# DeltaNet and low-rank mixer on one core: K of the later units loaded in 32x32 blocks, word pairs in the small triangles, and a new order of instructions

## The chip, the cores and the metric

The kernel runs on one core of a Trainium2 chip. A core has five engines that run beside each other, each in the order of its own instruction stream: TensorE (PE in the profile, its weight loads PEld), VectorE (DVE), ScalarE (ACT), GpSimd (POOL) and SyncE (SP). DMAs are issued from the streams of SP, POOL and ScalarE. TensorE writes to PSUM, and the other engines bring its results to SBUF. The metric is the device time of one execution in microseconds (us).

## The reference

Two blocks follow one another. The first is the delta rule for 4 batches, 8 heads, 768 tokens and a head size of 48: with k normalised, each token reads y from a 48 x 48 state and then corrects the state.

```python
for t in range(S):
    kt, vt, bt = (k_n[:, :, t], v[:, :, t], beta[:, :, t, None])
    y[:, :, t] = np.einsum('bhd,bhde->bhe', q[:, :, t], state)
    v_old = np.einsum('bhde,bhd->bhe', state, kt)
    state = state + bt[:, :, :, None] * np.einsum('bhd,bhe->bhde', kt, vt - v_old)
```

Its output, as x of shape (4, 768, 384), goes through a mixer over tokens of rank 32 and two dense layers with a residual:

```python
h = xt @ U @ V
u = x + h.transpose(0, 2, 1)
ch = np.maximum(u @ w_ch1, 0.0) @ w_ch2
return (u + ch).astype(np.float32)
```

## The kernel before

The tokens of a batch are cut in 12 chunks of 64. A **unit** is half a batch: 6 chunks of all 8 heads. There are 8 units, n = 0 to 7; two slots of SBUF hold the operands of the units in turn (`slots[n % 2]`), so that unit n can be loaded when unit n - 2 has been used up (the `need` at L302).

For a unit, `load` brings K, Q and V with tokens on the partitions (`kn`, `qn`, `vn`), and a second copy of K's odd heads on the other half of the partitions (`kz`, name 'z'). The products of a chunk with itself need K and Q turned, with the head's dimension on the partitions (`kq`). K of all units, and Q of units 0 and 1, are turned by TensorE with `transpose`, a half of a unit at a time (`turn`, 12 transposes, L221), and ScalarE copies the result out of PSUM (L412). Q of units 2 to 7 is loaded in blocks of 32 x 32 (16 columns in the second block of a head) by L320, and one VectorE instruction turns half a unit (`turn_blocks`, L421).

`products` multiplies K by K and K by Q (L432). From K by K, the two diagonal blocks of 32 x 32 of each 64 x 64 square go to `diag`: ScalarE writes the upper one (L436), and VectorE adds the lower one with a mask (L439). `blocks` then inverts the triangles. VectorE lays `diag` out with one triangle to each partition (L484), scales it, and substitutes column by column in `xt` (L493 and L494, a product and a subtraction in each of 31 steps; in units 0 to 2 the triangles are split once more, so there are 15 steps). L498 transposes the result back into `zz`, L505 turns its blocks, and small matmuls on 32x32 tiles of the array (L586 to L599, "joins") complete the 64 x 64 inverse in `pg`.

`recur` runs through the chunks of a batch in order. Each chunk needs the state before it, and sums the new state on VectorE (L745). `put` writes y to X. The mixer of a batch follows in three groups of 256 tokens: `front` (L948, L1074), `wide` (first dense layer, L1151 on the whole array or L209 in four quarters) and `narrow` (second layer, with seven products in place of eight, L1239 or L209). The last batch's first layer is done for all its tokens with fifteen products in place of eighteen (L929). The weights are converted by VectorE and ScalarE at the start (L834 to L843).

Each of these parts is a Python generator. It yields before each step, naming the step's engine and, for TensorE, the kind of array tile (`mode`: F whole array, H half of the rows, Q quarters, J 32x32 tiles, T column strips). The string `ORDER` names the generators by number, one token for each step, and `run` advances them in that order. Each engine's instructions stand in this order, so ORDER fixes what waits behind what. A token with the letter q picks the quarter form of a dense step, and digits after a dot pick the PSUM banks.

## Time and profile before

| | us |
|---|---|
| median of 3 runs | 578.34 |
| lowest and highest | 577.12 and 578.95 |
| profiled execution | 580.21 |
| its span, first to last instruction | 578.5 |
| TensorE busy | 542.4 |
| VectorE busy | 417.7 |
| ScalarE busy | 239.6 |
| POOL busy | 112.2 |

The page has busy times of the engines, the span in 40 slices, the chain of work that ended last, groups of equal instructions and DMA issues. The trace can be asked for the same by stage, and for single instructions. A group's row gives the line, engine and operation, the output and input tile, shapes and count, and then the busy time in us, the mean of one instruction in ns, and the engine's idle time ahead of the group. TensorE runs each fp32 matmul of the program as two in the profile, while a transpose is one. Durations of single matmuls overlap, so TensorE is read by distances from start to start.

### The profile page before, as it was taken

The page shows a single profiled execution, that of the slowest core. Times are in us where ns is not written, and L with a number is a line of the kernel's source. Part 1 is how long each engine was busy: PE and PEld are TensorE (multiplying, and loading weights), DVE is VectorE, ACT ScalarE, POOL GpSimd, SP SyncE. Part 2 cuts the span into 40 slices and gives each one's busy share as a digit, 9 for nine tenths or more (in the row PEclk, how much of TensorE's full clock was granted, in tenths as well). Part 3 has the DMA queues.
Part 4 walks back from the last instruction along what each step waited for, and adds up shares of the span by engine and source line. Part 5 has one row for each costly group of instructions (what it writes and reads, how often), then busy time and mean ns, then how long its engine had stood idle before and what let it go on. Part 6 is the DMA issues. An engine that isn't in the chain of part 4 may idle for free.

```text
span 578.5 us, 24970 instructions
## 1 busy us (share of the span) xinstructions
PE 542.4 (94%) x11205; PEld 457.4 (79%) x11205; DVE 417.7 (72%) x1018; ACT 239.6 (41%) x515; POOL 112.2 (19%) x193
## 2 busy tenths in 40 slices
PE   4476899999999999999999999999999999999997
PEld 4476787669789788789879977989889769656997
DVE  5799876889899337999898789998733345556532
ACT  2777787533422554146135333522352321435100
POOL 8041133530201350501107205120010000000000
PEclk9999559999999999999999999999999999999999
DMA  9977565440200150610405315020000000000001
GB/s 139 189 161 199 147 181 112 73 87 2 71 14 2 25 106 8 117 32 2 87 7 87 84 22 93 6 68 3 31 3 2 32 2 1 27 0 1 27 15 42
DMA packets 73835, 33.37 MB, mean 58 GB/s; under 512 B 60416, under 2 KB 71808, under 8 KB 73728
## 3 DMA queue, kind: packets, MB, share of 16 engines
q1 hardware_dynamic: 66400, 23.21, 18.4%
q0 software_dynamic: 5728, 8.27, 7.0%
q8 instruction: 88, 1.44, 1.1%
q10 hardware_dynamic: 1600, 0.30, 0.3%
q14 instruction: 19, 0.16, 0.1%
HBM read 27.03 MB, written 4.72 MB: 55 GB/s over the span
## 4 chain that ended last, share of the span: by engine, by line
PE 85%; DVE 6%; DMA 2%; ACT 2%; issue 2%; SPq 1%; ACTq 0%; DVEq 0%
PE P L1239 25%; PE P L1151 15%; PE P L209 10%; PE P L929 7%; PE P L432 4%; PE P L976 3%; PE P L653 2%; PE P L711 2%; PE P L646 2%; PE P L739 2%; PE P L698 2%; DMA slot<-in_k_dram 2%; PE P L221 1%; PE P L948 1%; PE P L1074 1%
## 5 line engine op out<-in xcount | busy, mean ns | idle before, releaser
L1151 PE MATMUL P<-ut,w_sb 128*128 128x256 f32 x384 | 88.0, 384 | 0.0
L1151 PEld LDWEIGHTS P<-ut,w_sb 128*128 128x128 f32 x384 | 71.4, 190 | 10.5 <-issue 0.6
L1239 PE MATMUL P<-w_sb,hs 128*128 128x192 f32 x456 | 79.1, 329 | 0.1
L1239 PEld LDWEIGHTS P<-w_sb,hs 128*128 128x128 f32 x456 | 74.2, 190 | 2.4 <-issue 1.4
L494 DVE TENSOR_TENSOR xt<-xt,prod 128x112 f32<-128x112 f32 (+21 forms) x200 | 64.6, 323 | 6.9
L493 DVE TENSOR_TENSOR prod<-gs,xt 128x112 f32<-128x112 f32 (+21 forms) x200 | 63.7, 318 | 3.7
L1185 DVE TENSOR_TENSOR X<-X,P 128x192 f32<-128x192 f32 x85 | 29.5, 349 | 42.9 <-PE P L1239 39.5
L1121 ACT ACTIVATE hs<-P 128x512 f32<-128x512 f32 x48 | 28.7, 598 | 66.3 <-PE P L1151 50.5
L209 PE MATMUL P<-ut,w_sb 64*64 64x256 f32 x768 | 51.8, 382 | 0.0
L1239 PE MATMUL P<-w_sb,S 128*128 128x192 f32 x240 | 41.9, 329 | 0.0
L432 PE MATMUL P<-slot 48*64 48x64 f32 x1536 | 33.3, 243 | 9.1 <-ACT slot L412 7.8
L636 ACT COPY X<-P 64x192 f32<-64x192 f32 x96 | 30.1, 314 | 25.1 <-PE P L653 23.7
L327 POOL DMA_DIRECT2D slot<-in_k_dram x44 | 29.7, 678 | 55.6 <-PE P L739 54.8
L432 PEld LDWEIGHTS P<-slot 48*64 48x64 f32 x1536 | 30.4, 156 | 12.3 <-ACT slot L412 8.6
L1239 PEld LDWEIGHTS P<-w_sb,S 128*128 128x128 f32 x240 | 38.9, 190 | 1.1 <-issue 0.6
L320 POOL DMA_DIRECT2D slot<-in_q_dram x48 | 29.6, 621 | 42.5 <-DVE z L729 25.2
L616 POOL MEMSET slot<- 32x384 f32 x32 | 13.2, 412 | 118.6 <-PE P L587 117.4
L612 ACT COPY slot<-zz 32x384 f32<-32x384 f32 x64 | 32.6, 509 | 4.3 <-DVE zz L568 1.7
L1239 PE MATMUL P<-w_sb,slot 128*128 128x192 f32 x180 | 30.4, 327 | 0.9 <-DVE X L1185 0.9
L209 PEld LDWEIGHTS P<-ut,w_sb 64*64 64x64 f32 x768 | 25.6, 133 | 7.1 <-issue 0.6
L914 DVE TENSOR_TENSOR slot<-slot,P 128x384 f32<-128x384 f32 x36 | 19.1, 552 | 16.3 <-PE P L929 15.4
L1239 PEld LDWEIGHTS P<-w_sb,slot 128*128 128x128 f32 x180 | 29.3, 190 | 1.7 <-DVE X L1185 1.5
(185 smaller groups left out, 1001.3 us busy)
## 6 DMA issues: line engine op xcount, KB each, us to landing
w_sb<-in_moe_w_ch_dram SPq DMA_DIRECT2D x14, 384.0 KB, 5.9
out_dram<-X SPq DMA_DIRECT2D x22, 192.0 KB, 2.0
slot<-in_k_dram SPq DMA_DIRECT2D x48, 72.0 KB, 4.0
slot<-in_k_dram POOLq DMA_DIRECT2D x44, 72.0 KB, 3.7
slot<-in_v_dram SPq DMA_DIRECT2D x32, 72.0 KB, 3.6
slot<-in_v_dram POOLq DMA_DIRECT2D x32, 72.0 KB, 3.4
X<-in_moe_w_ch_dram SPq DMA_DIRECT2D x6, 384.0 KB, 5.2
wide<-in_moe_w_ch_dram SPq DMA_DIRECT2D x4, 384.0 KB, 4.9
```

The source lines that it names most:

```text
L209: nc.tensor.matmul(to[half(g)], w[half(r), half(g)], x[half(r)], start=start, stop=stop, skip_group_check=True)
L320: queue.dma_start(out=blocked(n)[quarter(2 * par + y), j, g, :, 0:cols.stop - cols.start], in_=of[:, :, cols])
L327: queue.dma_start(out=t[half(1 - g if name == 'z' else g), :, to, 0:D], in_=src[b, 4 * g + s, hf * UC * L:(hf + 1) * UC * L, :].rearrange( ...
L432: nc.tensor.matmul(p_g[half(g ^ par * i), par, c], kq[rows, c, j, 0, half(g)], kq[rows, c, j, i, half(g)], start=True, stop=True)
L493: nc.vector.tensor_tensor(out=prod, in0=gb[:, :, j:j + 1, j + 1:].to_broadcast([128, split, m, w]), in1=xb[:, :, 0:m, j:j + 1].to_broadcas ...
L494: nc.vector.tensor_tensor(out=xb[:, :, 0:m, j + 1:], in0=xb[:, :, 0:m, j + 1:], in1=prod, op=ALU.subtract)
L612: nc.scalar.copy(pg[quarter(i), :, at, :, a:a + BK], cut(zc, h)[quarter(i)].rearrange('p r (c j) t -> p r c j t', j=2))
L636: nc.scalar.copy(x[half(c % 2), c // 2, 4 * D * g:4 * D * (g + 1)].rearrange('p (j r d) -> p r j d', r=2, d=D), states(p_y)[half(g)])
L929: nc.tensor.matmul(banks[x], w1_sb[:, 4 * a[0] + e, a[1]] if isinstance(a, tuple) else w1_mixes[a][:, e], tokens(*t) if isinstance(t, tupl ...
L1151: nc.tensor.matmul(p_f[:, x], w(x, t), ut[:, t], start=t == 0, stop=t == KT - 1)
L1185: nc.vector.tensor_tensor(out=to, in0=to, in1=p, op=ALU.add)
L1239: nc.tensor.matmul(to, of[0], of[1], start=of[2], stop=of[3], skip_group_check=True)
```

## The change

K of units 2 to 7 is loaded a second time, in 32x32 blocks (name 'kb', 16 DMAs for a unit), into the place that `pg` takes later, and VectorE turns it, half a unit at a time, as it does Q. TensorE's transposes of K and ScalarE's copies for these units are gone. The plain load of K puts the odd heads on the other half of the partitions, so that the second copy ('z', 4 DMAs for a unit) is not loaded for these units. The copy of the products into `pg` waits until both halves of K are turned.

`diag` and `zc` hold the triangles of two heads as adjacent words (`r` innermost), and with them the lines that write and read them; L484 and L498 then step over pairs of words. The substitution works on `xt` with its two axes exchanged. From unit 3 on (`LIGHT`), ScalarE writes both diagonal blocks, the lower one with two copies of 32 partitions, in place of a masked write by ScalarE and two masked additions by VectorE. Steps of `norms` and of the substitution that were issued together are steps of their own in ORDER, and the diagonal of `xt` is written by a product in place of a copy. ORDER is new as a whole.

The diff, with unchanged lines and most of ORDER left out:

```diff
@@ -37,6 +37,7 @@
+    LIGHT = 3
@@ -50,98 +51,107 @@
-    0 1 0 149 1 0 1 37 0 1 2 2 21 147 21 37 14.0 36 37 36 22 36 201 201 22 36 39 15.1 38 37 38 39 148 202.2
 ...
-    711 711
+    0 1 0 150 1 149 0 1 2 0 1 37 37 36 37 36 22 14.0 36 22 36 2 213 213 21 39 2 38 37 15.1 21 39 38 39 214.2
 ...
+    706 706 702 707 700 703 708 703 709 709 704 710 710 698 711 711
@@ -249,17 +259,20 @@
-        diag = slot[:, 6144:6144 + BK * BK].rearrange('p (q t) -> p q t', t=BK)
+        diag = slot[:, 6144:6144 + BK * BK].rearrange('p (e t r) -> p e t r', t=BK, r=2)
 ...
-    def blocked(n):
-        return slots[n % 2][:, 7680:9216].rearrange('p (j g x t) -> p j g x t', j=2, g=2, t=BK)
+    def blocked(n, i):
+        return slots[n % 2][:, 7680:9216] if i else slots[n % 2][:, 4608:6144]
+
+    def in_blocks(n, i):
+        return blocked(n, i).rearrange('p (j g x t) -> p j g x t', j=2, g=2, t=BK)
 ...
-        nc.gpsimd.memset(units[i][6][:, CS:], 0.0)
+        nc.gpsimd.memset(units[i][6][:, CS // 2:], 0.0)
@@ -274,7 +287,7 @@
-    zc = zz[:, 0:CS * BK].rearrange('p (q t) -> p q t', t=BK)
+    zc = zz[:, 0:CS * BK].rearrange('p (e t r) -> p r e t', t=BK, r=2)
@@ -297,8 +310,10 @@
-        t, src = dict(k=(kn, k), q=(qn, q), v=(vn, v), z=(kz, k))[name]
+        t, src = dict(k=(kn, k), q=(qn, q), v=(vn, v), z=(kz, k), kb=(None, k))[name]
 ...
+        if name == 'z' and n >= NU:
+            return
@@ -310,21 +325,21 @@
-            if name == 'q' and n >= NU:
+            if name == 'kb' or name == 'q' and n >= NU:
 ...
-                        queue.dma_start(out=blocked(n)[quarter(2 * par + y), j, g, :, 0:cols.stop - cols.start], in_=of[:, :, cols])
+                        queue.dma_start(out=in_blocks(n, int(name == 'q'))[quarter(2 * par + y), j, g, :, 0:cols.stop - cols.start], in_=of[:, :, cols])
 ...
-                queue.dma_start(out=t[half(1 - g if name == 'z' else g), :, to, 0:D], in_=src[b, 4 * g + s, hf * UC * L:(hf + 1) * UC * L, :].rearrange('(c t) d -> t c d', t=L))
+                queue.dma_start(out=t[half(1 - g if name == 'z' or (name == 'k' and n >= NU and s % 2) else g), :, to, 0:D], in_=src[b, 4 * g + s, hf * UC * L:(hf + 1) * UC * L, :].rearrange('(c t) d -> t c d', t=L))
@@ -351,7 +366,7 @@
-            nc.scalar.copy(out=rows[:, :, 2 * UC * r:2 * UC * r + 2 * UC].rearrange('p b (c j) -> p c b j', c=UC), in_=p_bt.rearrange('p c (b j r) -> p r c b j', b=B, j=2)[:, r])
+            nc.scalar.copy(out=rows[:, :, 0:CS].rearrange('p b (c j r) -> p r c b j', c=UC, j=2)[:, r], in_=p_bt.rearrange('p c (b j r) -> p r c b j', b=B, j=2)[:, r])
@@ -371,18 +386,22 @@
+        yield op('dve')
 ...
+        yield op('dve')
 ...
+        yield op('dve')
 ...
-        nc.vector.tensor_copy(out=xt.rearrange('p s t -> p (s t)')[:, 0:BK * BK:BK + 1], in_=cp[:, n % 2])
+        yield op('dve')
+        nc.vector.tensor_tensor(out=xt.rearrange('p s t -> p (s t)')[:, 0:BK * BK:BK + 1], in0=rec, in1=betas[:, hf, b], op=ALU.mult)
 ...
-        nc.vector.tensor_tensor(out=vn.rearrange('p c (r j) d -> p r c j d', r=2), in0=vn.rearrange('p c (r j) d -> p r c j d', r=2), in1=rows[:, 0:CS].rearrange('p (r c j) -> p r c j', r=2, c=UC)[:, :, :, :, None].to_broadcast([128, 2, UC, 2, D]), op=ALU.mult)
+        nc.vector.tensor_tensor(out=vn.rearrange('p c (r j) d -> p r c j d', r=2), in0=vn.rearrange('p c (r j) d -> p r c j d', r=2), in1=rows[:, 0:CS].rearrange('p (c j r) -> p r c j', r=2, c=UC)[:, :, :, :, None].to_broadcast([128, 2, UC, 2, D]), op=ALU.mult)
@@ -390,9 +409,6 @@
-            if n >= NU and i == 0 and (j == 0):
-                yield op('pool')
-                nc.gpsimd.memset(diag[:, CS:], 0.0)
@@ -414,13 +430,16 @@
-        def turn_blocks(j):
-            yield landed('q', n, j)
-            yield op('dve')
-            of = blocked(n)[:, j].rearrange('p g (c u) t -> p c g (u t)', u=2)
-            nc.vector.transpose(kq[:, :, j, 1].rearrange('p c (g t) -> p c g t', g=2), of)
-            emitted(('turned', n, 1, j))
-            begin(products(j, 1))
+        def turn_blocks(j, i):
+            yield landed(('kb', 'q')[i], n, j)
+            if i == 0 and j == 0:
+                yield op('pool')
+                nc.gpsimd.memset(diag[:, CS // 2:], 0.0)
+            yield op('dve')
+            of = in_blocks(n, i)[:, j].rearrange('p g (c u) t -> p c g (u t)', u=2)
+            nc.vector.transpose(kq[:, :, j, i].rearrange('p c (g t) -> p c g t', g=2), of)
+            emitted(('turned', n, i, j))
+            begin(products(j, i))
@@ -431,14 +450,22 @@
-                to = diag[:, 0:CS].rearrange('p (r c j) t -> p r c j t', r=2, c=UC)[:, :, :, j]
-                yield op('act')
-                nc.scalar.mul(to, p_g[:, :, :, 0:BK], even[:, 0:1])
-                for r in range(2):
-                    yield op('dve')
-                    nc.vector.scalar_tensor_tensor(out=to[:, r], in0=p_g[:, r, :, BK:L], scalar=even[:, 1:2], in1=to[:, r], op0=ALU.mult, op1=ALU.add)
+                to = diag[:, 0:CS // 2].rearrange('p (c j) t r -> p r c j t', j=2)[:, :, :, j]
+                if n >= LIGHT:
+                    yield op('act')
+                    nc.scalar.copy(to, p_g[:, :, :, 0:BK])
+                    for r in range(2):
+                        yield op('act')
+                        low = quarter(2 * r + 1)
+                        nc.scalar.copy(to[low], p_g[low, :, :, BK:L])
+                else:
+                    yield op('act')
+                    nc.scalar.mul(to, p_g[:, :, :, 0:BK], even[:, 0:1])
+                    for r in range(2):
+                        yield op('dve')
+                        nc.vector.scalar_tensor_tensor(out=to[:, r], in0=p_g[:, r, :, BK:L], scalar=even[:, 1:2], in1=to[:, r], op0=ALU.mult, op1=ALU.add)
 ...
-                yield (need(*[('diag', n, y) for y in range(2)]) if n == 0 else [])
+                yield need(*[('diag', n, y) for y in range(2) if n == 0], *[('turned', n, 0, y) for y in range(2) if n >= NU])
@@ -452,7 +479,7 @@
-            begin(turn_blocks(j) if i and n >= NU else turn(name, t, j, i))
+            begin(turn_blocks(j, i) if n >= NU else turn(name, t, j, i))
@@ -481,7 +508,7 @@
-        nc.vector.transpose(gs[:, 0:BK], diag.rearrange('p q t -> p t q'))
+        nc.vector.transpose(gs[:, 0:BK].rearrange('p t (e r) -> p t e r', r=2), diag.rearrange('p e t r -> p t e r'))
@@ -489,20 +516,24 @@
-            prod = single.tile([128, split, m, w], FP32, name='prod', tag='prod')
-            nc.vector.tensor_tensor(out=prod, in0=gb[:, :, j:j + 1, j + 1:].to_broadcast([128, split, m, w]), in1=xb[:, :, 0:m, j:j + 1].to_broadcast([128, split, m, w]), op=ALU.mult)
-            nc.vector.tensor_tensor(out=xb[:, :, 0:m, j + 1:], in0=xb[:, :, 0:m, j + 1:], in1=prod, op=ALU.subtract)
+            prod = single.tile([128, split, w, m], FP32, name='prod', tag='prod')
+            nc.vector.tensor_tensor(out=prod, in0=gb[:, :, j, j + 1:, None].to_broadcast([128, split, w, m]), in1=xb[:, :, j:j + 1, 0:m].to_broadcast([128, split, w, m]), op=ALU.mult)
+            yield op('dve')
+            nc.vector.tensor_tensor(out=xb[:, :, j + 1:, 0:m], in0=xb[:, :, j + 1:, 0:m], in1=prod, op=ALU.subtract)
 ...
-        nc.vector.transpose(zz[:, 0:BK * BK].rearrange('p (q t) -> p t q', t=BK), xt[:, 0:BK].rearrange('p s t -> p t s'))
+        nc.vector.transpose(zz[:, 0:BK * BK].rearrange('p (e t r) -> p t e r', t=BK, r=2), xt[:, 0:BK].rearrange('p t (e r) -> p t e r', r=2))
 ...
-            nc.vector.transpose(cut(zn, h), cut(zc, h))
+            nc.vector.transpose(cut(zn, h), thirds(h))
+
+        def thirds(h):
+            return zc[:, :, 6 * h:6 * h + 6]
@@ -547,7 +578,7 @@
-                        nc.tensor.matmul(p_e[to, y // 6, y % 6], of, zc[rows, e, SB:BK], start=True, stop=True)
+                        nc.tensor.matmul(p_e[to, y // 6, y % 6], of, zc[rows, e // 12, e % 12, SB:BK], start=True, stop=True)
@@ -564,7 +595,7 @@
-                    to = cut(zc, h)[:, r, :, SB:BK]
+                    to = thirds(h)[:, r, :, SB:BK]
@@ -572,7 +603,7 @@
-                return zc[rows, 12 * r + 2 * c + j]
+                return zc[rows, r, 2 * c + j]
@@ -609,7 +640,7 @@
-                nc.scalar.copy(pg[quarter(i), :, at, :, a:a + BK], cut(zc, h)[quarter(i)].rearrange('p r (c j) t -> p r c j t', j=2))
+                nc.scalar.copy(pg[quarter(i), :, at, :, a:a + BK], thirds(h)[quarter(i)].rearrange('p r (c j) t -> p r c j t', j=2))
@@ -685,7 +716,7 @@
-            yield need(*([('ready', n, h)] if ahead else [('gram', n), ('scaled', n)]), *landed('z', n))
+            yield need(*([('ready', n, h)] if ahead else [('gram', n), ('scaled', n)]), *(landed('z', n) if ahead else landed('k', n)))
@@ -736,7 +767,7 @@
-                    nc.tensor.matmul(states(p_s)[half(par, D), g, j], kz[at, cu, j] if par else kn[at, cu, 2 * j, 0:D], zs[c][at, 2 * par + j], start=True, stop=True)
+                    nc.tensor.matmul(states(p_s)[half(par, D), g, j], kz[at, cu, j] if par and n < AHEAD else kn[at, cu, 2 * j + par, 0:D], zs[c][at, 2 * par + j], start=True, stop=True)
@@ -1282,14 +1313,17 @@
-        for k in range(3):
-            begin(added(k))
+        for x in range(3):
+            begin(added(x))
 ...
+        for n in range(NU, N):
+            for some in ((0,), (1,)):
+                begin(load(n, 'kb', some))
 ...

```

## The prediction

> **What bounds the kernel now.** I read the page's busy times and slices first, then the chain of waits, then the busy times by stage, and last the groups and single instructions of the parts that the change touches. From the page (busy us, slices in tenths, chain by engine):

> ```profile
> span 578.5 us, 24970 instructions
> PE 542.4 (94%) x11205; PEld 457.4 (79%) x11205; DVE 417.7 (72%) x1018; ACT 239.6 (41%) x515; POOL 112.2 (19%) x193
> ...
> PE   4476899999999999999999999999999999999997
> ...
> DVE  5799876889899337999898789998733345556532
> ...
> PEclk9999559999999999999999999999999999999999
> ...
> PE 85%; DVE 6%; DMA 2%; ACT 2%; issue 2%; SPq 1%; ACTq 0%; DVEq 0%
> ```

> TensorE is the chain for 85% of the span and is full from the sixth slice on; VectorE's 6% lies at the start. Busy times by stage (columns: PE, PEld, DVE, ACT, POOL, granted clock, DMA share, GB/s) show the three regimes:

> ```profile
> 20.00:62.00 42.00, 28.08 (x907) 25.31 (x909) 40.07 (x118) 28.83 (x55) 9.08 (x15) 0.94 0.78 184
> 62.00:98.00 36.00, 33.41 (x1016) 29.25 (x1013) 26.30 (x49) 29.61 (x56) 12.59 (x20) 0.69 0.57 150
> 98.00:545.00 447.00, 441.76 (x8901) 365.85 (x8901) 329.32 (x788) 171.93 (x390) 76.84 (x129) 1.00 0.17 36
> ```

> From 20 to 62 us VectorE is busy 40.07 of 42 us and sets the pace. From 62 to 98 TensorE takes over (33.41 of 36), much of it at a reduced clock. From 98 to 545 TensorE is busy 441.76 of 447: only 5.2 us are idle, so there only TensorE's own work counts. Work on ScalarE, POOL and the queues costs time only if something arrives late.

> **TensorE loses the transposes of K.** The turn of K for units 2 to 7 was 6 units x 2 halves x 12 = 144 transposes. The groups between 98 and 545 us hold exactly these, and single instructions (start, duration) give the pace in context:

> ```profile
> L221 PE MATMUL P<-ident,slot 64*128 64x64 f32 x144 | 6.8, 228 | 0.1
> ```
> ```profile
> 209.30 0.59 PE L221 MATMUL P<-ident,slot 64*128 64x64 f32 x12
> 209.91 0.45 PE L698 MATMUL P<-s,slot 48*64 48x48 f32 x16
> ...
> 353.44 0.96 PE L221 MATMUL P<-ident,slot 64*128 64x64 f32 x24
> 354.49 2.14 PE L948 MATMUL P<-X,u_sb 128*32 128x384 f32 x24
> ```

> One block of 12 holds the engine 0.61 us from its start to the next start, two in a row 1.05 us. The 144 have 6.8 us of busy time, all of it in the saturated stage: **-6.8 us**. Bounds: if all went at the pace of the double block, 6 x 1.05 = 6.3; if all stood alone, 12 x 0.61 = 7.3.

> **The new order of TensorE switches array tiles more often.** TensorE uses whole-array, quarter, half-row and 32x32 tiles. Grouping each program's matmuls into runs of one tile kind gives 167 runs before and 177 after. The runs of half-row transposes fall from 19 to 11, so the other kinds gain 18 runs; of 166 and 176 switches, those that touch no half-row run rise from 129 to 155: 26 more. A switch is priced by whole-array matmuls between quarter work:

> ```profile
> 99.42 1.13 PE L976 MATMUL P<-ut,w_sb 128*128 128x256 f32 x4
> 100.48 0.45 PE L646 MATMUL P<-s,slot 48*64 48x48 f32 x16
> ...
> 102.04 0.70 PE L976 MATMUL P<-ut,w_sb 128*128 128x256 f32 x2
> 102.67 0.45 PE L653 MATMUL P<-z,slot 64*64 64x48 f32 x16
> ```

> Four take 1.06 us from start to next start, two 0.63: 0.215 us each, and 0.63 - 2 x 0.215 = 0.20 for going in and out, 0.1 a switch. 26 x 0.1 = **+2.6 us**. It is 0 if they fall where the engine waits anyway (28.08 of 42 us busy at 20 to 62), and 2.6 if all fall later; I take 2.6, because the saturated stage is most of the span.

> **VectorE: word pairs.** The groups this part and the next need (busy us, mean ns, idle before):

> ```profile
> L498 DVE STREAM_TRANSPOSE zz<-xt 128x1024 f32<-128x1024 f32 x8 | 16.7, 2085 | 0.1
> L484 DVE STREAM_TRANSPOSE gs<-slot 128x1024 f32<-128x1024 f32 x8 | 15.6, 1946 | 0.3
> L439 DVE SCALAR_TENSOR_TENSOR slot<-P,even,slot 128x192 f32<-128x192 f32 x32 | 12.1, 410 | 7.2 <-ACT slot L436 7.2
> L505 DVE STREAM_TRANSPOSE zz<-zz 128x384 f32<-128x384 f32 x22 | 12.1, 569 | 0.4
> L421 DVE STREAM_TRANSPOSE slot<-slot 128x768 f32<-128x768 f32 x12 | 11.6, 969 | 0.7 <-DMA slot<-in_q_dram 0.5
> L412 ACT COPY slot<-P 128x768 f32<-128x768 f32 x18 | 14.1, 799 | 4.0 <-PE P L221 3.8
> L603 ACT ACTIVATE slot<-P 32x384 f32<-32x384 f32 x32 | 15.3, 481 | 12.9 <-PE P L599 12.4
> L327 POOL DMA_DIRECT2D slot<-in_k_dram x44 | 29.7, 678 | 55.6 <-PE P L739 54.8
> L320 POOL DMA_DIRECT2D slot<-in_q_dram x48 | 29.6, 621 | 42.5 <-DVE z L729 25.2
> ```

> L505 and L421 go along unbroken words: (969 - 569) / (768 - 384) = 1.04 ns an element, so 1,024 elements would take 969 + 256 x 1.04 = 1,236 ns. L484 and L498 step 32 words per element and take 1,946 and 2,085. After the change they step over pairs of adjacent words. No row has that access, so the gain lies between 0 and the unbroken rate, 0.71 and 0.85 us each. I take the unbroken rate, because a pair halves the number of long steps and the strided side is then only one of the two.

> [...] No run so far shows a pair.

> It counts only in the first stage, where VectorE is the bound. Its transposes there, by single instruction:

> ```profile
> 14.71 1.89 DVE L484 STREAM_TRANSPOSE gs<-slot 128x1024 f32<-128x1024 f32 x1
> ...
> 30.70 2.05 DVE L498 STREAM_TRANSPOSE zz<-xt 128x1024 f32<-128x1024 f32 x1
> 32.63 1.92 DVE L484 STREAM_TRANSPOSE gs<-slot 128x1024 f32<-128x1024 f32 x1
> ```
> ```profile
> 63.07 2.15 DVE L498 STREAM_TRANSPOSE zz<-xt 128x1024 f32<-128x1024 f32 x1
> ```

> 0.71 + 0.85 + 0.71 = 2.3 us before 62 us, and 0.85 more as TensorE takes over: 2.3 to 3.1, taken as **-2.7 us**; its low end is 0, if the weights' DMA sets this stage after all (DMA share 0.78).

> **What I cost at nothing, and what covers it.** After 98 us VectorE (329 of 447 us), ScalarE (172) and POOL (77) lie beside TensorE.
> - VectorE: 12 more block turns x 0.969 = +11.6 us; 20 multiply-adds fewer in units 3 to 7 x 0.41 = -8.2; the sixteen transposes 8 x 0.71 + 8 x 0.85 = -12.5. Together -9.1 us, 2.7 of them already counted. Products of K now wait for VectorE's turn instead of a TensorE transpose and ScalarE's copy.
> - The single instructions that the reorganised steps now issue apart, the diagonal written as a product rather than a copy, and the substitution's two operations, whose operands only change places, keep count and size: 0.
> - ScalarE: 12 copies fewer (L412) x 0.80 = -9.6; 20 copies of 32 partitions x 384 more, priced by L603: 20 x 0.48 = +9.6. Zero.
> - POOL: 48 issues of blocks of K x 0.621 = +29.8, 12 issues of the second copy of K fewer x 0.678 = -8.1: +21.7 us on 112. SP gains 36 issues likewise. What stands behind them in the same order are the loads of Q and V and POOL's clearing of xt and of the lower blocks. Cover gone, they are the first rival.

> **The sum.** -6.8 + 2.6 - 2.7 = **-6.9 us**. The profiled execution took 580.2 us, its span of 578.5 and 1.7 around it; it would come to 573.3. It lies 1.9 us over the median of the three runs, 578.3, which gives **571.4 us**. About 0.3% (1.7 us) is what a measurement of this kernel can tell from no change.

> **Rival 1, slower: the blocks of K arrive late.** A turn of K could start after four issues on each queue; now it waits for eight. Before, unit 4's loads and turn (issue, and landing as a median):

> ```profile
> 202.81 2.63 SPq L327 DMA_DIRECT2D slot<-in_k_dram  x4
> 205.54 2.11 SPq L320 DMA_DIRECT2D slot<-in_q_dram  x4
> ```
> ```profile
> slot<-in_k_dram POOLq DMA_DIRECT2D x44, 72.0 KB, 3.7
> ...
> slot<-in_q_dram POOLq DMA_DIRECT2D x24, 48.0 KB, 3.2
> ```

> The turn began at 209.30, 6.5 us after the first issue: 2.6 of issuing, 3.7 of landing, almost nothing spare. Eight issues take 8 x 0.621 = 5.0 us, so a turn can begin 2.3 us later for the same release. If all six units meet TensorE's order without slack, 6 x 2.3 = 13.8 us come back as waits of TensorE: 571.4 + 13.8 = **585 us**. It decides from 6.9 / 6 = 1.15 us a unit. Against it: unit 4's products stand as far behind the release as before in the new order (by the rows' paces some 12 us of TensorE work), and blocks of Q, of the same shape, land as fast as K's rows.

> [...]

> **Rival 2, faster still: the idle time goes and the clock comes early.** The stage of the reduced clock:

> ```profile
> 58.00:82.00 24.00, 21.05 (x691) 19.56 (x681) 19.31 (x46) 19.14 (x39) 2.85 (x7) 0.50 0.57 162
> ```

> If the new order also removed the 5.2 us of idle time and the switches cost nothing: 571.4 - 5.2 - 2.6 = **563.6 us**. A clock granted 5 us earlier would give up to 5 x 0.88 x 0.5 = 2.2 more. For it: the order is new throughout. Against: nothing in the trace says that the clock comes sooner.

> **Rival 3, no change: the saved TensorE time turns into waits.** TensorE's fill between a unit's products of K and its joins covers VectorE's substitution, and VectorE is 74% busy there. If the chain on VectorE ends last instead, the 4.2 us net on TensorE come back, and if the weights set the start, the 2.7 too: **578 us**. The 5.2 us of idle time in 447 speak against a chain that near.

> **Chances.** Forecast 0.56, with a range of its own of 567 to 576; rival 1 0.17; rival 2 0.14; rival 3 0.13, a third of it below the bound of 0.3% by a part of the gains. Faster: 0.56 + 0.14 + 0.04 = 0.74; same 0.08; slower 0.17 + 0.01 = 0.18. The range reaches from rival 2 with an earlier clock, 562, to just short of rival 1's full price, 583.

> **What would show it.** Right: no L221 group on the K slots between 98 us and the end but the 60 on X; the two transposes of 1,024 at some 1.24 us; TensorE busy in the saturated stage some 4 us less, with idle time near 5 us; unit 2's first work on TensorE 2 to 3 us earlier. Wrong: transposes that stay near 2 us; TensorE waiting for "slot<-in_k_dram" or for the turn line of VectorE in units 2 to 7; a reduced clock past 82 us.

## The result, and the profile after

The changed kernel takes 580.84 us (median of 6, 579.27 to 582.44); beside it the kernel before took 578.02 (577.12 to 579.92). The ratio is 1.005, with a 95% interval of 1.0026 to 1.0073: slower by about half a per cent, where 571.4 and a gain were forecast. The time lies inside the range of 562 to 583, on the other side of no change. Measured twice more, the same kernel gave 583.29 and 582.59, ratios of 1.0078 (1.005 to 1.0106) and 1.0051 (1.0027 to 1.0075). Its single times scatter from 579.3 to 585.8, those of the kernel before from 577.1 to 582.0.

The page of the changed kernel: span, busy times, slices of TensorE and of the granted clock, and the chain by engine. The profiled execution took 582.44.

```profile
span 580.0 us, 24828 instructions
PE 538.4 (93%) x11061; PEld 449.4 (77%) x11061; DVE 406.9 (70%) x1010; ACT 239.7 (41%) x523; POOL 134.0 (23%) x229
...
PE   5666788999999999999999999999999999999997
...
PEclk9998669999989999999999999999999999999999
...
PE 82%; DVE 6%; issue 4%; DMA 3%; ACT 2%; SPq 1%; POOL 0%; DVEq 0%; POOLq 0%
```

TensorE is 4.0 us less busy and the span is 1.5 us longer. Two things are new: "issue", time in which TensorE waits for nothing that the trace shows, went from 2% to 4% of the chain, and the clock has a dent in the twelfth slice (160 to 174 us), long after the start. The stages, with the columns of the prediction's table:

```profile
20.00:62.00 42.00, 28.49 (x945) 25.56 (x949) 40.16 (x121) 29.03 (x56) 9.63 (x15) 0.91 0.80 194
62.00:98.00 36.00, 31.01 (x991) 26.46 (x985) 23.93 (x46) 28.06 (x54) 14.51 (x23) 0.78 0.59 140
98.00:545.00 447.00, 438.86 (x8745) 359.10 (x8746) 318.93 (x775) 172.55 (x399) 96.22 (x162) 1.00 0.20 40
```

From 98 to 545 us TensorE is 2.9 us less busy, but idle for 447 - 438.86 = 8.1 us instead of 5.2. What it waits for there (line, releaser, us in total, times, longest):

```profile
PE P L742 <- DVE rest L735: 1.5, 5, 0.4
PE P L451 <- issue: 1.4, 1, 1.4
PE P L770 <- ACT z L745: 1.4, 4, 0.5
```

The kernel before has, in the same stretch:

```profile
PE P L646 <- DVE s L745: 0.9, 3, 0.4
PE P L739 <- ACT z L714: 0.7, 2, 0.5
PE P L711 <- DVE rest L704: 0.5, 1, 0.5
```

Two of the changed kernel's waits are small ones inside the recurrence (L742 and L770, before L711 and L739), which grew; that of L646 nearly went (0.2 us at L677). L451 has one single stop without a releaser. The groups that the change meant to alter came out as meant (busy, mean ns, idle before):

```profile
L440 DVE STREAM_TRANSPOSE slot<-slot 128x768 f32<-128x768 f32 x24 | 23.0, 966 | 0.3
...
L526 DVE STREAM_TRANSPOSE zz<-xt 128x1024 f32<-128x1024 f32 x8 | 10.0, 1245 | 0.2
L511 DVE STREAM_TRANSPOSE gs<-slot 128x1024 f32<-128x1024 f32 x8 | 9.9, 1232 | 1.6 <-ACT slot L460 1.4
...
L231 PE MATMUL P<-ident,slot 64*128 64x64 f32 x96 | 7.2, 319 | 7.8 <-DMA slot<-in_k_dram 7.2 <-issue 0.6
```

The 144 transposes are gone, VectorE's 24 block turns wait 0.3 us in all, and the word pairs go at 1.23 and 1.25 us instead of 1.95 and 2.09. So the work that was to go is gone, and something took the time back.

To see where, the table compares the start of the same matmul. Each column is the time in the kernel before, each entry how much later (+) or earlier (-) the other execution is there: three executions of the changed kernel, and experiments told of below. The reference is the profiled execution of before, which at 580.21 is itself 0.6 to 2.2 us above that kernel's medians on the chips used, so changes along a row say more than its level.

| us in before | 103 | 131 | 155 | 170 | 251 | 350 | 545 |
|---|---|---|---|---|---|---|---|
| after | -1.9 | -2.3 | -2.4 | +0.8 | +0.3 | +0.5 | +1.4 |
| after_again | -2.7 | -3.1 | -3.2 | -1.9 | -2.5 | -1.9 | -0.8 |
| after_beside | -3.3 | -3.7 | -3.6 | -2.3 | -2.8 | -2.0 | -0.9 |
| after_split | -2.9 | -3.3 | -3.1 | -2.6 | -3.2 | -2.9 | -1.8 |
| pairs_only | -1.0 | -1.3 | -1.4 | -1.4 | -1.5 | -1.7 | -2.0 |
| old_order | -2.5 | -3.4 | +1.4 | +2.7 | +6.2 | +6.4 | +12.7 |

The changed kernel is ahead at 103 us and loses 1.9 to 3.3 us from there to 545, where 3.0 of the 4.2 us were to be won (24 of the 144 transposes stood at 98 to 102 us, ahead of the first column). 1.3 to 3.2 of it go at one place, between 155 and 170 us. The traces after_again and after_beside are of executions of 579.64 and 579.39 us, the fastest of theirs; what their medians of 583.29 and 582.59 lose beyond that is not in the table.

### The profile page after: what moved, and what is told of

It is laid out like the page before. It is cut to its first block, busy times and chain, and to the rows that moved or that the text cites. A ratio compares the mean times of both kernels' runs of the same rounds, so it can differ in the third digit from the quotient of the medians.

```text
span 580.0 us, 24828 instructions
## 1 busy us (share of the span) xinstructions
PE 538.4 (93%) x11061; PEld 449.4 (77%) x11061; DVE 406.9 (70%) x1010; ACT 239.7 (41%) x523; POOL 134.0 (23%) x229
## 3 DMA queue, kind: packets, MB, share of 16 engines
q8 instruction: 86, 1.41, 1.0%
HBM read 28.80 MB, written 4.72 MB: 58 GB/s over the span
## 4 chain that ended last, share of the span: by engine, by line
PE 82%; DVE 6%; issue 4%; DMA 3%; ACT 2%; SPq 1%; POOL 0%; DVEq 0%; POOLq 0%
PE P L1270 25%; PE P L1182 15%; PE P L219 10%; PE P L960 7%; PE P L451 3%; PE P L1007 2%; PE P L742 2%; PE P L677 2%; PE P L729 2%; PE P L770 2%; PE P L684 2%; DMA slot<-in_k_dram 1%; PE P L1105 1%; PE P L979 1%; DVE xt L522 1%
## 5 line engine op out<-in xcount | busy, mean ns | idle before, releaser
L1182 PE MATMUL P<-ut,w_sb 128*128 128x256 f32 x384 | 91.0, 391 | 0.8 <-issue 0.5
L1182 PEld LDWEIGHTS P<-ut,w_sb 128*128 128x128 f32 x384 | 72.2, 193 | 12.6 <-issue 1.8
L643 ACT COPY slot<-zz 32x384 f32<-32x384 f32 x64 | 34.4, 542 | 12.1 <-DVE zz L599 6.1
L451 PE MATMUL P<-slot 48*64 48x64 f32 x1536 | 33.4, 241 | 6.3 <-ACT slot L428 4.6
L451 PEld LDWEIGHTS P<-slot 48*64 48x64 f32 x1536 | 30.1, 153 | 10.1 <-ACT slot L428 5.0
L776 DVE TENSOR_TENSOR s<-s,P 128x192 f32<-128x192 f32 x40 | 14.0, 350 | 32.1 <-PE P L770 25.6
L342 POOL DMA_DIRECT2D slot<-in_v_dram x32 | 21.1, 664 | 50.2 <-DVE s L776 17.0
```

The costliest lines, as they stand in the source:

```text
L451: nc.tensor.matmul(p_g[half(g ^ par * i), par, c], kq[rows, c, j, 0, half(g)], kq[rows, c, j, i, half(g)], start=True, stop=True)
L643: nc.scalar.copy(pg[quarter(i), :, at, :, a:a + BK], thirds(h)[quarter(i)].rearrange('p r (c j) t -> p r c j t', j=2))
L1182: nc.tensor.matmul(p_f[:, x], w(x, t), ut[:, t], start=t == 0, stop=t == KT - 1)
```

## The stop of TensorE, seen in the trace

TensorE in the changed kernel, by start and duration (in brackets the idle time ahead):

```profile
161.96 0.99 PE L595 MATMUL P<-zz 32*32 32x16 f32 x96
162.89 0.80 PE L451 MATMUL P<-slot 48*64 48x64 f32 x36
165.10 1.09 PE L451 MATMUL P<-slot 48*64 48x64 f32 x58 [1.42 <-issue]
...
166.40 6.27 PE L1182 MATMUL P<-ut,w_sb 128*128 128x256 f32 x20
```

96 joins (L595, of unit 2) and 96 products of Q of unit 3 follow one another, each with its own weight load: 384 instructions in 2.65 us, not counting the stop of 1.42 us that breaks them after 132 matmuls. In all sixteen traces every stop over 0.5 us without a releaser comes at the same place of TensorE's own instruction stream: counting matmuls, weight loads and semaphore instructions, at 193 to 195 in each 256 (this one behind 7,361 of them, 28 x 256 + 193; those of the kernel before at 78 and 89 us behind 3,265 and 3,777, also at 193). The queue that I take to go with it, by the counts below, stands among the page's DMA queues (packets, MB, share), first over the whole span, then from 162 to 163.7 us alone:

```profile
q8 instruction: 86, 1.41, 1.0%
```
```profile
q8 instruction: 1, 0.02, 3.5%
```

1.41 MB in 86 packets are 16 KB each, and 22,122 matmuls and weight loads by 86 are 257: about one packet for 256 instructions (in the kernel before 88 packets for 22,410, 255 each). The packet in this window ran from 162.87 to 163.83, and TensorE resumed 1.3 us after its end. Behind 98 us, TensorE has only two such stops in this trace, this one of 1.42 us and one of 0.5 at a dense group (L1182); that TensorE runs dry here, among the smallest matmuls of the kernel, is read from the order in time. A fast stretch alone is not enough: the kernel before runs 192 joins of unit 2 (384 instructions) from 144.45 to 146.80 us without such a stop. There a packet had started at 143.61 us, ahead of the joins; here it started 0.9 us behind their beginning. What happened next is the half clock (columns as above, for 163 to 167 and 167 to 171 us):

```profile
163.00:167.00 4.00, 2.58 (x114) 2.35 (x115) 3.68 (x10) 2.06 (x5) 0.00 (x0) 0.96 0.19 25
167.00:171.00 4.00, 4.00 (x13) 3.21 (x13) 2.72 (x7) 0.36 (x2) 0.00 (x0) 0.61 0.01 2
```

13 dense matmuls in 4 us at a clock of 0.61; at a clock of 1.00 they take 0.22 us each from start to start (24 in 5.38 us, in after_again). In the repetitions the stop was 1.18 and 1.17 us long and the clock stayed at 1.00; the 24 dense matmuls behind it took 5.38 us there and 7.07 here. With the longer stop, that is the 2 us by which the first row of the table falls behind the next two at 170.

## Experiments: which part of the change costs what

**The kernel itself, again.**

> The changed kernel unaltered, once more, for a second profile of it. Theory O (the new order loses what the edits gain, whatever the clock does): again 580 to 582 us, 0.3 to 0.7% over the kernel before, also in an execution without a reduced clock at 167 to 171 us. Theory C (the reduced clock at 167 to 171 us is the loss, about 2 us of it, plus the pause before it): the reduced stretch comes back at the same place, and executions without it are at 578 or below.

Measured 583.29 us, ratio 1.0078 (1.005 to 1.0106). The slowdown repeats.

**Word pairs alone**, in the order of before: TensorE still turns K.

```diff
-            begin(turn_blocks(j) if i and n >= NU else turn(name, t, j, i))
+            begin(turn_blocks(j, i) if i and n >= NU else turn(name, t, j, i))
-        nc.vector.transpose(gs[:, 0:BK], diag.rearrange('p q t -> p t q'))
+        nc.vector.transpose(gs[:, 0:BK].rearrange('p t (e r) -> p t e r', r=2), diag.rearrange('p e t r -> p t e r'))
+    LIGHT = 99
```

> The kernel before with its own order and its own TensorE turn of K; only the diagonals and the inverted blocks lie in pairs of words, and the two transposes go along pairs (the substitution has its two axes swapped as well). My prediction's term: two shorter transposes a unit, 2.3 to 3.1 us less in the first stage and nothing after it: 575 to 576 us. Rival (the first stage is set by something else, weights or a later wait): 577.5 to 578.5 us, with VectorE idle more before 60 us.

Measured 577.63 us (12 runs) against 578.51, ratio 0.9981 (0.9965 to 0.9997): 0.9 us faster, a third of the 2.7. The transposes are as fast as in the changed kernel:

```profile
L513 DVE STREAM_TRANSPOSE zz<-xt 128x1024 f32<-128x1024 f32 x8 | 9.9, 1235 | 0.1
L499 DVE STREAM_TRANSPOSE gs<-slot 128x1024 f32<-128x1024 f32 x8 | 9.8, 1227 | 0.3
```

Here a pair goes at the rate of unbroken words: 1,235 and 1,227 ns, with 1,236 worked out from the prediction's rows. What does not follow is the time at the end. The gain is there at first: from 20 to 40 us, where two of the transposes stand (0.71 + 0.85 us by the prediction), this kernel gains 1.6 us on the kernel before, and the changed kernel 1.4, while before_s24 below, without pairs, gains nothing there. By 80 us it is gone again: 0.8 us ahead at 20, 2.4 at 40 and 1.9 at 62, this kernel is 0.5 behind at 80. TensorE's waits from 20 to 98 us in this kernel:

```profile
PE P L664 <- issue: 4.0, 3, 2.3
PE P L757 <- issue: 1.6, 2, 1.3
```

The kernel before had 0.7, 0.6 and 0.4 us of such waits there, the changed kernel 3.0 to 6.9 us in all in its three traces. TensorE, released sooner by VectorE, stops at its instruction loads, beside which the weights are still arriving (DMA share 0.81 from 20 to 62 us, 0.55 from 62 to 98). This is one execution of each; that it is the whole of the missing 1.8 us is argued, not shown. From 103 to 350 us the row of this kernel in the table hardly moves, as it should with an unchanged order.

**All edits in the order of before**, with each turn of K at the place that TensorE's turn had.

```diff
 ORDER (before's tokens; only the names that the added DMAs shift are renumbered)
+    LIGHT = 3
+            begin(turn_blocks(j, i) if n >= NU else turn(name, t, j, i))
```

> All edits of the change, but the instructions in the order of the kernel before: VectorE's turn of K stands where TensorE's stood, two block loads stand for each load of K's rows, and K's rows where the second copy stood. Theory O (the new order is what loses): the sum of my prediction comes out, 571 to 574 us. Theory W (the saved TensorE time turns into waits whatever the order): 577 to 580 us, TensorE's busy time about 7 us less than before and its idle time as much more. Rival 1 of the prediction (late blocks): TensorE waits for the DMA or for VectorE's turn in units 2 to 7, some 585 us.

Measured 592.42 us, ratio 1.0238 (1.0212 to 1.0264), 14.8 us more than word pairs alone in the same order. The two differ in the blocks of K and in who writes the diagonals (`LIGHT`); no run parts these in all units. VectorE, and below it TensorE, where the table's row jumps by 6 us:

```profile
361.29 0.98 DVE L433 STREAM_TRANSPOSE slot<-slot 128x768 f32<-128x768 f32 x1 [1.20 <-DMA slot<-in_k_dram]
...
363.87 0.98 DVE L433 STREAM_TRANSPOSE slot<-slot 128x768 f32<-128x768 f32 x1 [0.91 <-DMA slot<-in_k_dram]
...
367.78 0.55 DVE L1083 COPY tt<-P 128x384 f32<-128x384 f32 x1
```
```profile
363.00 2.18 PE L216 MATMUL P<-w_sb,hs 64*64 64x192 f32 x48
368.38 0.88 PE L1097 MATMUL P<-tt,v_sb 64*64 64x384 f32 x8 [3.20 <-DVE tt L1083]
```
```profile
370.00:374.00 4.00, 4.00 (x96) 3.29 (x92) 3.71 (x12) 0.35 (x1) 0.00 (x0) 0.67 0.00 0
```

The turn waits for its blocks twice (1.20 and 0.91 us) and itself takes twice 0.98. Behind it in VectorE's order stands the copy `tt` for the mixer, which has nothing to do with K; TensorE waits 3.20 us for it, and then runs 4 us at a clock of 0.67. At 131 to 155 us TensorE waits 1.7 us for VectorE's sum in X, ahead of which a turn of 0.97 us stands at 128.6 us, here without a wait for its blocks; how much of the 1.7 is the turn's is not shown. A stop at an instruction load follows (1.50 us, then a clock of 0.57 from 147 to 151 us). By the order of the streams, TensorE's turn, when late, delays TensorE's own order; VectorE's turn delays all that stands behind it in VectorE's, here `tt`, and with it TensorE by 3.20 us.

**TensorE's turn in the new order.**

```diff
-            begin(turn_blocks(j, i) if n >= NU else turn(name, t, j, i))
+            begin(turn_blocks(j, i) if i and n >= NU else turn(name, t, j, i))
-        if name == 'z' and n >= NU:
-            return
 ORDER: the twelve turns moved from VectorE's places to TensorE's
```

> The order of the changed kernel with TensorE's turn of K put back: 144 transposes and their 12 copies on ScalarE stand where VectorE's 12 turns stood, K is loaded in rows and twice, all else as changed. Theory N (the transposes are worth their 6.8 us in this order too, and it is the order that costs more than that): 586 to 590 us. Theory W (in this order something else ends last, so what TensorE saves is worth nothing): 581 to 583 us.

Measured 598.74 us, ratio 1.034 (1.0316 to 1.0363); the first turn of unit 4 overwrites one partial sum of the mixer's first dense layer, so this kernel does not compute the reference's output. It does not give the clean price of the transposes that it was made for: beside their own work, TensorE has waits that my placing of the turns brought in, for instance behind ScalarE's copy:

```profile
PE P L775 <- ACT slot L433: 1.1, 2, 0.9
```

With the others it gives a square: TensorE's turn 577.6 in the old order and 598.7 in the new, VectorE's turn 592.4 in the old and 580.8 to 583.3 in the new. Each order suits its own way of turning K, though the first corner lacks `LIGHT` and the second has the waits of my placing. With VectorE's turn, the new order is 9 to 11 us faster than the old one (by the ratios), so it wins back a good part of the 14.8 us, and not all.

**Blocks of K for unit 2 alone, and for units 2 and 7**, each with the word pairs in the order of before, and a few small matmuls at the start (below).

```diff
+    KB = (2,)
-            begin(turn_blocks(j, i) if i and n >= NU else turn(name, t, j, i))
+            begin(turn_blocks(j, i) if n in KB or (i and n >= NU) else turn(name, t, j, i))
```

> Word pairs in the order of before, K in blocks for unit 2 alone, and a shift by 44 (11 small matmuls), at which no 256 instructions after 98 us go by in under 3.2 us; with a shift by 104 the same kernel had four stops of 3.7 us after 98 us and started 1 to 2 us later. Theory F: no stop over 0.5 us after 98 us, and the end comes 1.0 to 1.2 us before that of the word pairs alone (two transposes of 12 taken away): 576 to 577 us. If it is 577.5 or more, unit 2's gain turns into waits even with the stops gone.

Measured 580.05 us (12 runs), ratio 1.0022 (1.0005 to 1.0039), 0.41% above word pairs alone. No stop over 0.5 us comes after 98 us, as expected, and the row of differences is flat from 103 us on (+2.2 to +2.1). The loss is in the start, where TensorE stops at four loads for 1.2 to 2.2 us (in a traced execution that is the slowest of the twelve). Behind the start the edit saves nothing either. The two transposes of unit 2 that TensorE loses were worth 1.2 us; VectorE's two turns now stand ahead of the sum of the state, `s`, and TensorE waits 1.19 and 0.59 us for it, first VectorE, then TensorE:

```profile
99.62 0.97 DVE L437 STREAM_TRANSPOSE slot<-slot 128x768 f32<-128x768 f32 x1
100.51 0.31 DVE L772 TENSOR_TENSOR s<-s,P 128x192 f32<-128x192 f32 x1
...
102.50 0.97 DVE L437 STREAM_TRANSPOSE slot<-slot 128x768 f32<-128x768 f32 x1
103.40 0.32 DVE L772 TENSOR_TENSOR s<-s,P 128x192 f32<-128x192 f32 x1
```
```profile
100.88 0.45 PE L749 MATMUL P<-s,slot 48*64 48x48 f32 x16 [1.19 <-DVE s L772]
...
103.77 0.45 PE L749 MATMUL P<-s,slot 48*64 48x48 f32 x16 [0.59 <-DVE s L772]
```

This is how a TensorE saving turns into a wait.

> As before with K in blocks for unit 7 too, whose turns stand later in VectorE's queue (4.5 and 3 us ahead of the products) and whose blocks are issued ahead of its rows; a shift by 28. In the run with all edits in the old order, unit 7 lost 6.4 us to a turn that waited for its blocks. Theory V (only where the turn stands matters): unit 7 gains another 1 to 1.2 us, 575 to 576.5 us, with a stop or two of up to 1 us from the shift taken off: 575.5 to 577.5. Theory W: the turn or its blocks make TensorE wait again at 355 to 365 us, 579 us or more.

Measured 583.58 us, ratio 1.0084 (1.0057 to 1.011). Unit 7 alone costs 4.5 us between 350 and 385 us, although its blocks were issued first and turned late:

```profile
363.38 1.81 PE L448 MATMUL P<-slot 48*64 48x64 f32 x96 [1.67 <-DVE slot L437]
```

TensorE waits for the turn itself, and a half clock follows (0.57 from 1 to 5 us behind the wait), worth about as much again. Whether the old order has a better place for this turn was not tried.

## Experiments: the stops

The theory that stops sit at fixed places of the instruction stream makes a forecast that no wait for data makes: instructions put in at the start move every later stop to another piece of work. The edit is a few small matmuls into an unused corner of PSUM; only their number differs. Each is an fp32 matmul and runs as two matmuls with two weight loads, 4 instructions (the six of before_s24 stand in its trace as 12 matmuls, and the pages count as many weight loads as matmuls, 11,061 of each in the changed kernel); the first four expectations below took it for 2, so that the shifts there are twice those named.

```diff
+    for _ in range(11):
+        nc.tensor.matmul(P[0:64, 7, 256:272], ident[0:64, 0:64], ident[0:64, 0:16], start=True, stop=True)
```

**11 in the changed kernel (44 instructions).**

> The changed kernel with 11 small matmuls of the identity ahead of TensorE's first transpose, while TensorE waits for K anyway. They move every later instruction of TensorE's stream 22 places on, and do nothing else. Theory F (TensorE's instructions are loaded 256 at a time; where 256 go by in under about 3.2 us the load comes late and TensorE stops at that place, and a stop of over about 1.4 us also costs some 4 us of half clock): the stop at 163 to 165 us inside the 96 products goes, no stop without a releaser is left after 98 us but small ones, no reduced clock past 98 us; 577 to 580 us, 1.5 to 4 us under the changed kernel. Theory O (the order of the work alone): the stop stays at the same product, and the time at 580.8 to 583.

Measured 584.6 us, ratio 1.0106 (1.0072 to 1.014): not faster, a miss. The stop at 163 us is gone: from 155 to 170 us this trace loses nothing, where the changed kernel lost 1.3 to 3.2. But others come up. Before 103 us they reach 1.85 us, and this trace is there 2.4 to 3.8 us behind the changed kernel's; later, one stands where a shift of 44 puts it:

```profile
394.13 0.40 PE L744 MATMUL P<-rest,slot 64*64 64x48 f32 x14
395.54 0.26 PE L744 MATMUL P<-rest,slot 64*64 64x48 f32 x2 [1.00 <-issue]
```

**74 in the kernel before (296), 58 in old_order (232), 26 beside unit 2's blocks (104).**

> The kernel before with 74 such small matmuls at its start, 148 places. Theory F: new stops at about 144, 164 and 268 us, 1 to 1.5 us each, which the kernel before does not have, and with them half clock for some us: 582 to 586 us. Theory O: no new stop, 578 to 579 us.

Measured 598.09 us, ratio 1.0332. The small matmuls took 0.107 us each and put off the start by 11 us, which spoils the time; a stop of 1.45 us stands at 179.4 us, inside unit 3's products, at the place that the true shift gives, not at those of the expectation. This bears on the place alone.

> All edits in the order of the kernel before, with 58 such small matmuls at its start, 116 places, at which by theory F no 256 instructions after 98 us go by in under 3.2 us. Theory F for the most of the 14.8 us that this order loses with the edits: 584 to 587 us and the stops at 145, 168, 238 and 389 us gone. Theory V (VectorE's turn of K stands in its queue ahead of work that TensorE waits for): the stops go, but the waits for L1208 at 132 us and L1083 at 365 us stay with their reduced clock, and the time stays at 588 us or more.

Measured 607.08 us, ratio 1.0469. The stops were to go and did not: new ones of 1.78, 1.72 and 1.46 us stand at the places that a shift of 232 gives. The two large waits for VectorE stay (1.7 and 3.5 us). Of the 14.7 us above old_order, 11 are there by 103 us, as the small matmuls put off the start.

> The kernel with word pairs in the order of before, and K in blocks for unit 2 alone; 26 small matmuls at the start make up for the 48 instructions that unit 2's transposes leave. Unit 2's TensorE transposes took 0.6 us each, two of them; in the run with all edits in the old order TensorE was 1.6 us ahead behind unit 2 and lost it only later. If one unit's gain comes through where nothing waits: 576 to 577 us, 1 to 1.5 us under the word pairs alone. Theory W (what TensorE saves turns into waits): 577.5 to 578.5.

Measured 589.55 us, ratio 1.0184, with five stops at the products of K and Q of 3.9 us in all, against none over 0.5 us with 44. Kernels that differ only in this shift lie 9.5 us apart (both against their own runs of before, 1.0184 and 1.0022); their two traces lie 6.1 apart, 5.7 of it behind 103 us.

**6 in the changed kernel and, as a control, in the kernel before (24).**

> The changed kernel with 6 small matmuls of the identity at its start, where TensorE waits for K. Each runs as two matmuls with a weight load apiece, four places of the stream, so this is a shift by 24 (11 of them gave 44). By the places at which the trace of the changed kernel shows 256 instructions gone by, a shift of 24 leaves no 256 after 98 us in under 3.2 us. Theory F: the stops at 163 to 165 us and at 375 us go and none over 0.5 us comes in their place; 1.9 us of stops and up to 2 us of half clock less: 577.5 to 580 us. Theory O (these stops are incidental): 580.8 to 583 us.

Measured 585.28 us, ratio 1.0126 (1.0096 to 1.0156). A miss: the place moves back by 12 matmuls, which still lies inside the products, and the stop even grew. More stops in the start (up to 1.67 us) leave this trace 2.8 to 4.2 us behind the changed kernel's at 103 us:

```profile
168.40 1.65 PE L453 MATMUL P<-slot 48*64 48x64 f32 x72 [1.85 <-issue]
```

> Control for the shifts: the kernel before with 6 small matmuls of the identity at its start, 24 places of the stream, at which by the places in its trace no 256 instructions after 98 us go by in under 3.2 us. If the small matmuls do no harm of their own: 577.5 to 580 us, no stop over 0.5 us after 98 us. If they do (a different clock or a later first stage): 581 us or more, with the loss ahead of 98 us; then the times of the shifted kernels are to be read from their stages after 98 us alone.

Measured 581.59 us, ratio 1.0049 (1.0027 to 1.007). The start is not delayed, but small stops of 0.4 to 0.7 us come up behind 98 us. So the order of before sits at a place of the stream that is better than the two others tried. Neither of the two shifts makes the changed kernel faster; every shift that was run costs.

**The stop alone taken away.** One group of dense matmuls (six in the trace, not the twelve of the expectation) is issued between the joins of unit 2 and unit 3's products of Q instead of a little later, so that nothing else in the stream moves.

```diff
-  ... 297 305 299.2 ...   (the token 305, a dense group, after the products)
+  305 ahead of the products of unit 3, after the joins of unit 2
```

> The changed kernel with one group of twelve matmuls of the first dense layer (L1182 in its numbering, about 1.06 us of work) issued between the joins of unit 3 (L595, 96 of 32x32) and its products of K and Q, instead of later. The number of instructions ahead of every other place stays. The theory that TensorE stops where 256 of its instructions go by in less time than their successors need to be loaded: the group makes room just where the trace of after stops 1.42 us (163.7 to 165.1) and the repetition 1.18 us; the stop falls to under 0.5 us, there is no half clock at 167 to 171, and the time is 1.2 to 3.5 us below that of the changed kernel beside it. The theory that the loss is the order as a whole, and the stop only a place where a delay shows that would come anyway: the stop moves or its gain is lost again before the end; within 0.8 us of the changed kernel.

> The changed kernel itself, for the comparison on one chip: a ratio of 1.004 to 1.009 to the kernel before, as in its earlier runs; a stop of 1.1 to 1.5 us at 163 us, and past 98 us some 2 us of waits in the recurrence more than before.

Measured 580.59 us (12 runs) for the split and 582.59 (12 runs) for the changed kernel beside it; by drawing from the two sets of runs again, their means differ by 2.4 us, with an interval of 1.0 to 3.7. Ratios to before 1.0019 (0.9999 to 1.004) and 1.0051. First the changed kernel beside it, then the split:

```profile
161.73 0.80 PE L451 MATMUL P<-slot 48*64 48x64 f32 x36
163.70 1.09 PE L451 MATMUL P<-slot 48*64 48x64 f32 x58 [1.17 <-issue]
```
```profile
161.30 0.99 PE L601 MATMUL P<-zz 32*32 32x16 f32 x96
162.22 1.56 PE L1188 MATMUL P<-ut,w_sb 128*128 128x256 f32 x6
163.71 2.02 PE L457 MATMUL P<-slot 48*64 48x64 f32 x95
```

The stop is gone, its time is not lost again before the end (the rows of the table keep their distance), and the gain of 2.0 to 2.4 is more than the 1.17 us of this execution, as it would be if some executions also pay the half clock, which is argued. The theory of the loads holds. It is also not the whole: the split is not faster than before, but 2.0 us above it by the medians and 1.1 by the ratio, whose interval just reaches no change.

## Why the prediction was wrong

**The transposes of K, -6.8: right where they are removed.** The sum over TensorE's starts behind 98 us gives -6.8 for L221 in the changed kernel and in the split.

**Word pairs, -2.7: mis-sized.** The instruction came out as the upper end said (1,232 and 1,245 ns), and the two between 20 and 40 us save there what was counted. The step that failed is that what VectorE saves in the first stage is saved for good: alone, the pairs gave 0.9 us, as TensorE then stops at its instruction loads.

**Tile switches, +2.6: the price held, the term did not.** The dense groups of the first layer came in 19 runs before and in 25 in the split, and took 86.16 and 87.32 us from start to start (without a stop of 0.72 us that falls into one of them): 0.19 us for each further run, where 0.20 was priced for going in and out. But the term was all that the new order was to cost TensorE in its own work, and that step failed. Between the same two matmuls at 103 and 545 us, which leaves 120 of the 144 transposes to be saved, the split compares with the kernel before as follows:

| us, from 103 to 545 | forecast | split |
|---|---|---|
| transposes of K | -5.6 | -5.59 |
| TensorE's other work | +2.6 | +4.72 |
| waits for data over 0.15 us | 0 | +1.33 |
| stops at instruction loads | 0 | +0.59 |
| sum | -3.0 | +1.05 |

Of the 4.7, 1.2 are the six further runs of the first dense layer, 1.0 the matmuls on quarters (L209 of the kernel before, in 67 runs in place of 74) and 0.7 those for the new state (its L739); the rest is spread. What makes these slower is not shown. The changed kernel itself, in after_again, has +4.8, +1.2 and +1.5, in sum +1.9. This compares one execution of each.

**"What I cost at nothing": the step that failed.** Nothing on VectorE, ScalarE or the queues was too long in sum, and the block turns in the new order hardly wait. But I asked only whether work is covered on average, not what the new order makes of each wait: waits for data grew from 3.5 to 4.8 us, those in the recurrence from 3.0 to 4.0. And the reading "only TensorE's own work counts from 98 us on" left out TensorE's instruction stream as something that can be late. That cost 1.2 to 1.4 us at 163, some 0.5 to 0.7 at 375, and the half clock in one of the three traces 1.7 more.

**The rivals.** Rival 3, 578, was nearest in time: the saved TensorE time does not reach the end, though less than half of it went into waits, and those not into VectorE's chain of substitution; the nearness is in part luck. Rival 1's mechanism shows in old_order, by way of VectorE's queue: blocks that are late by 1.20 and 0.91 us. That its price of 13.8 us lies near the 14.8 there is luck, as these hold over 4 us of stops at instruction loads and two half clocks. The new order avoids the wait for blocks. Rival 2's premise is refuted: the idle time grew from 5.2 to 8.1 us.

**The signs named beforehand.** No L221 group on K, transposes at 1.24 us, and an early recurrence (1.9 to 3.3 us at 103) came; TensorE's idle time near 5 us did not, its busy time fell by 2.9 us in place of 4, and "a reduced clock past 82 us" came, at 167 to 171.

**What stays open.** The three traces of the changed kernel end between 579.4 and 582.4 us, while its runs reach 585.8 and two of its three medians lie above 582.5; in what the slower ones lose more time no trace shows. The stop is the one part of the loss that was taken away by an edit. That the rest is TensorE's own work and small waits is read from single traces, and how the split's distance to before divides between the start and the order isn't settled, as the start scatters by more than 1 us from one execution to the next. Of all kernels run here, word pairs in the old order is the only one below before, 0.998.

## What to carry to other kernels

An order that was settled with one engine's waits in it is part of the kernel: an operation moved to another engine should be priced together with what stands behind it in the new engine's queue, and in old_order such edits cost 14.8 us where the operation's own time was 6.8. Before long runs of very small matmuls are put back to back, count instructions: here 384 of them in 2.65 us could outrun their own loading, and one dense group between two such runs took the stop away, at 0.2 us for one more run. When a stop without a releaser is suspected, a few harmless instructions at the start tell it apart from a wait for data, because the stop moves to other work and the wait doesn't: in old_shift three new stops of 1.46 to 1.78 us came up, while the two large waits for VectorE stayed, at 1.7 and 3.5 us.

## What was not expected of the hardware

Such a stop can bring on the half clock. Behind 98 us, none of 1.00 to 1.38 us did. Of eight of 1.42 to 1.85 us, five did (clock 0.56 to 0.64 over the 3 or 4 us behind them: 1.42, 1.46, 1.50, 1.72 and 1.85) and three did not (1.45, 1.58 and 1.78, clock 1.00). It need not be a stop at a load: the waits of 1.67 us in k27_s28 and 3.20 in old_order were followed by it, one of 3.46 in old_shift was not. Stops as close as 1.45 us (shift_bad) and 1.46 (old_shift) had different outcomes; what decides between them no run here shows.
